# Blocks of 128 rows by seven products in both layers of a routed two-layer network

## The chip, the cores and the metric

The kernel runs on one core of a Trainium2 chip. The metric is the device time of one execution in microseconds; the kernel before takes 626.38 us, the median of 3 runs (626.19 to 627.47).

## What is computed

An attention with a window of 64 positions feeds a network of eight experts. Each of the 4608 rows (8 sequences of 576) goes through the two matrices of one expert: its own choice, or the expert of the row before where a gate says so. Cut to what matters here:

```python
attn = softmax(q @ k.T / 8, masked to the last 64 positions); x = attn @ v   # x: 8 x 576 rows of 512
logits = x @ w_gate                                     # 8 experts
e = argmax(logits[b, s]) or the row before's e          # by a gate on x @ w_local
h = np.maximum(x[b, s] @ w1[e], 0.0)                    # 512 -> 1024
out[b, s] = p[e] * (h @ w2[e])                          # 1024 -> 512, p = softmax(logits)
```

All of it is in fp32.

## The kernel before

Attention and most of the choice of experts come first; the expert stage writes its first h at 137.9 us of the span and fills the rest. Rows are sorted by expert into blocks that each belong to one expert: blocks of 256 rows, and for what an expert has left over, blocks of 128, 64 and 32 rows. A block's rows are gathered by index (GpSimd issues these transfers), its two weight matrices of 2 MB each come over SyncE's queue into a ring of four tiles, and its results are scattered by index to the output.

In method `run` a fixed list gives the order of blocks. With the number of rows in brackets, after three blocks of 256 it is: 256, 256, [128], 256, [32], 256, [128], 256, 256, [128], 256, [32], 256, [128], 256, 256, [64], 256, 256, 256, [64]. So four blocks of 128 rows are computed, each with a block of 256 before it and one behind it. A 32-row block is not computed on its own: its products are put between those of the 256-row block ahead of it.

A block of 256 rows does each layer by seven products of half-size matrices instead of eight (the Winograd form of Strassen's scheme). In each layer the stationary and the moving operand are cut into quarters; VectorE makes four sums of quarters on either side, TensorE does seven products, and ScalarE and VectorE put the products together:

- `prepare` makes four sums of x (`xs`, by `right`) and four of W1 (`ws`, by `left`), the last two of W1 later (`rest`, `more`);
- `big_hidden` starts with `prepare2`, four sums of W2 (again named `ws`, L1326), then does the products L1363. ScalarE saves three interim results (`keep`, L1370); VectorE's adds (L1375) and ScalarE's relu (L1376) make h. The fifth and the seventh product accumulate into the same PSUM tile `px`, which the second VectorE add reads in between. At the end `halves` makes four sums of h (`hs`, L1312);
- `big_result` does the products L1414, ScalarE scales interim results (`kept`, L1420), VectorE finishes the output (L1425).

`hooks` are pieces of other work that `big_result` calls between its products: the rest of the next block's sums, or the products of a 32-row block and the turning of the rows of the block behind that. Turning is VectorE's transpose, L1283.

A block of 128 rows does its layers directly: in `hidden` 32 matmuls of 128 columns (L1514) and two relus (L1525 on VectorE, L1527 on ScalarE), in `result` 8 matmuls of 512 columns (L1566). Blocks of 64 rows use the same methods with 64-wide column halves of the array, two matmuls side by side (L1514 at 64x64, L1544).

In this stage the order on each engine is the order of the code: a manual schedule covers TensorE, VectorE, ScalarE, GpSimd and SyncE, so an engine that waits holds everything behind it. `pace` ties a gather or a scatter to the end of a product; `late` keeps a block's last scatter back into the next block.

## Time and profile before

| | |
|---|---|
| median of 3 runs | 626.38 us (626.19 to 627.47) |
| the profiled execution: its time, its span | 627.78 us, 626.0 us |
| granted TensorE clock, mean | 0.999 |
| PE busy | 600.5 us (96%) |
| VectorE (DVE) busy | 403.2 us (64%) |
| ScalarE (ACT) busy | 200.5 us (32%) |
| GpSimd (POOL) busy | 271.4 us (43%) |
| HBM traffic | 264 GB/s over the span |

The span runs from the first to the last instruction of one profiled execution. In a row of the timeline stand the start in us, the length, the engine, the line, the operation, what it writes and reads, the shape, the number of records, and in brackets the idle time ahead of it and what ended it. An fp32 matmul leaves two records, so the 32 matmuls of L1514 in one block are x64. Matmuls are pipelined: the time that a group takes from the array is read from its start to the next group's start, not from its length. Lengths on VectorE and ScalarE overlap by some 0.1 us when the next instruction needn't wait for the one before.

### The profile page before, as it was taken

How to read it: one execution, taken by the hardware profiler on the slowest of the kernel's cores; microseconds unless marked ns; L12 is line 12 of the kernel's file. 1: busy time of each engine (PE TensorE's matmuls, PEld its weight loads, DVE VectorE, ACT ScalarE, POOL GpSimd, SP SyncE). 2: the span in 40 equal slices, each digit the busy share in tenths (PEclk: the TensorE clock that was granted, in tenths of full speed). 3: DMA queues.
4: the chain of work that ended last, by engine and by line, in shares of the span. 5: the costliest groups of instructions: out<-in, count | busy, mean ns of one | idle time of the engine just before them, and what ended most of it. 6: DMA issues, size and time to landing. Idle time of an engine off the chain costs nothing. (4 is left out here: it accounts for less than half of the span.)

```text
span 626.0 us, 15072 instructions
## 1 busy us (share of the span) xinstructions
PE 600.5 (96%) x6253; PEld 528.9 (84%) x6253; DVE 403.2 (64%) x757; ACT 200.5 (32%) x368; POOL 271.4 (43%) x261
## 2 busy tenths in 40 slices
PE   7888988999999999999999999999999999999995
PEld 6677766788889999979899799978997998999994
DVE  6567579888996767347381885183926763886730
ACT  3766755722382232203130123112221322123120
POOL 4432111622102567437146775175275866452001
PEclk9999999999999999999999999999999999999999
DMA  8999998787945557476967866687768656955601
GB/s 328 401 415 407 365 378 284 273 304 250 385 153 186 190 210 281 170 272 246 394 245 259 321 198 217 230 314 300 299 239 316 256 189 223 403 193 208 233 18 40
DMA packets 31880, 165.80 MB, mean 265 GB/s; under 512 B 10531, under 2 KB 12217, under 8 KB 22586
## 3 DMA queue, kind: packets, MB, share of 16 engines
q1 hardware_dynamic: 20394, 135.54, 58.6%
q0 software_dynamic: 11408, 29.20, 13.0%
q8 instruction: 51, 0.84, 0.5%
q14 instruction: 27, 0.22, 0.1%
HBM read 145.52 MB, written 19.59 MB: 264 GB/s over the span
## 5 line engine op out<-in xcount | busy, mean ns | idle before, releaser
L1184 POOL DMA_INDIRECT xg<-xs,g x118 | 134.2, 1138 | 46.0 <-issue 25.3
L1494 POOL DMA_INDIRECT out_dram<-y,idx x36 | 41.1, 1142 | 161.3 <-DVE y L1425 68.5
L1414 PE MATMUL hp<-ws,hs 128*128 128x256 f32 x384 | 88.9, 380 | 0.0
L1414 PEld LDWEIGHTS hp<-ws,hs 128*128 128x128 f32 x384 | 72.5, 190 | 10.9 <-issue 1.2
L1363 PE MATMUL hp<-xs,ws 128*128 128x128 f32 x672 | 79.7, 275 | 0.0
L1363 PEld LDWEIGHTS hp<-xs,ws 128*128 128x128 f32 x672 | 77.3, 192 | 0.1
L1425 DVE SCALAR_TENSOR_TENSOR y<-hp,pws,kept 128x256 f32<-128x256 f32 x48 | 23.2, 482 | 68.2 <-issue 41.2
L1514 PE MATMUL hp<-xt,w 128*64 128x64 f32 (+2 forms) x640 | 66.2, 276 | 0.0
L1514 PEld LDWEIGHTS hp<-xt,w 128*128 128x128 f32 (+1 forms) x640 | 60.8, 170 | 4.1 <-issue 0.7
L1414 PE MATMUL hp<-w,h 128*128 128x256 f32 x256 | 60.5, 379 | 0.0
L1375 DVE TENSOR_TENSOR h<-hp,keep 128x512 f32<-128x512 f32 x42 | 28.6, 689 | 43.9 <-PE hp L1363 43.1
L1363 PEld LDWEIGHTS hp<-xt,w 128*128 128x128 f32 x448 | 53.2, 192 | 2.7 <-issue 2.3
L1363 PE MATMUL hp<-xt,w 128*128 128x128 f32 x448 | 54.7, 275 | 0.0
L394 PEld LDWEIGHTS sp<-w 64*64 64x64 f32 x1296 | 39.1, 135 | 16.2 <-issue 11.2
L1414 PEld LDWEIGHTS hp<-w,h 128*128 128x128 f32 x256 | 47.3, 190 | 5.7
L425 ACT ACTIVATE p<-sp 128x512 f32<-128x512 f32 x72 | 39.1, 596 | 37.1 <-PE sp L394 34.8
L440 PE MATMUL xo<-vb,p 128*64 128x74 f32 (+1 forms) x576 | 44.0, 228 | 6.9 <-DVE x L450 3.0
L394 PE MATMUL sp<-w 64*64 64x128 f32 (+1 forms) x1296 | 45.1, 267 | 5.7 <-issue 4.5
L430 DVE TENSOR_TENSOR p<-p,mask 128x1024 f32<-128x1024 f32 x29 | 35.8, 1235 | 22.4 <-ACT p L425 22.3
L1184 POOL DMA_INDIRECT pws<-xw,gx x40 | 44.3, 1107 | 13.2 <-issue 8.5
L440 PEld LDWEIGHTS xo<-vb,p 128*64 128x64 f32 x576 | 38.3, 136 | 12.6 <-issue 5.2
L1376 ACT ACTIVATE h<-h 128x512 f32<-128x512 f32 x42 | 26.3, 630 | 60.1 <-DVE h L1375 60.1
(287 smaller groups left out, 977.5 us busy)
## 6 DMA issues: line engine op xcount, KB each, us to landing
w<-in_w_dram SPq DMA_DIRECT2D x22, 2048.0 KB, 9.4
w<-in_w1t_dram SPq DMA_DIRECT2D x20, 2048.0 KB, 8.7
w<-in_kq_dram SPq DMA_DIRECT2D x17, 1024.0 KB, 11.2
w<-in_w_dram SPq DMA_DIRECT2D x24, 512.0 KB, 8.5
xs<-x POOLq DMA_DIRECT2D x9, 1024.0 KB, 5.9
va<-in_v_dram SPq DMA_DIRECT2D x5, 1184.0 KB, 7.5
vtt<-in_vt_dram SPq DMA_DIRECT2D x5, 1024.0 KB, 6.2
va<-in_v_dram SPq DMA_DIRECT2D x3, 1040.0 KB, 15.5
```

The source lines that it names most:

```text
L394: nc.tensor.matmul(sp[j][c * WIN:(c + 1) * WIN, a:b], lhsT=kt[h, hp, block * WIN:(block + 1) * WIN], rhs=qt[h, hp, a:b], start=not biased, ...
L425: nc.scalar.activation(p[:, j], sp[j], Act.Exp, scale=DH ** -0.5)
L430: masked.append(nc.vector.tensor_tensor(p, p, m.to_broadcast([P, 2, SC]), op=Alu.mult))
L440: nc.tensor.matmul(xo[par * WIN:(par + 1) * WIN, j, s * VW:s * VW + n], lhsT=p[:, j, b * WIN:(b + 1) * WIN], rhs=w[:, s, 2 * hp + j, :n], ...
L1184: return self.nc.gpsimd.indirect_dma_start(out=out, out_offset=None, in_=table[:rows, :], in_offset=bass.IndirectOffsetOnAxis(ap=idx, axis=0))
L1363: mm = nc.tensor.matmul(out[:, m, :], lhsT=a[:, kk, m * P:(m + 1) * P], rhs=b[:, kk, :], start=start and m + kk == 0, stop=stop and (m, kk ...
L1375: nc.vector.tensor_tensor(o, x, y, op=add)
L1376: nc.scalar.activation(o, x if y is None else o, Act.Relu)
L1414: mm = nc.tensor.matmul(out, lhsT=a[:, m, :], rhs=b[:, m, :], start=start and m == 0, stop=stop and m == FK // 2 - 1, skip_group_check=True)
L1425: nc.vector.scalar_tensor_tensor(o, x, pw[i], y2, Alu.mult, Alu.add)
L1494: return self.nc.gpsimd.indirect_dma_start(out=self.out[:, :], out_offset=bass.IndirectOffsetOnAxis(ap=st["idx"][:, s:s + 1], axis=0), in_ ...
L1514: mm = nc.tensor.matmul(hp[a, i, :], lhsT=st["w1"][:, kk, m * P:(m + 1) * P][:, a], rhs=st["xt"][:, kk, :n], start=(kk == 0), stop=(kk == ...
```

## The change

Blocks of 128 rows (`n < KINDS[1]`) now have `fast1` and `fast2` set too, so both their layers go by seven products. Where rows and hidden columns are halved, a block of 128 rows leaves 64 on the stationary or the moving side, so the products run on 64-wide column halves of the array (`c` in `big_hidden`). The second layer has a method of its own, `small_result`: in its first three passes (`r1` to `r3`) the two halves of the array do two different products at once, in the fourth (`r4`) they share the seventh. Results in the upper partitions are moved by ScalarE copies, eight small VectorE adds put the output together, and ScalarE scales it by the gate's weight at the end (`store`). The hooks of `small_result` turn and prepare the block behind.

The second part concerns a 256-row block that stands behind a 32-row block (`after`): W2's fourth sum is left out of `prepare2` and made behind h's four sums.

```diff
-        st.update(..., fast1=len(slots) == 2 and n not in PLAIN1,
-                  fast2=len(slots) == 2 and n not in PLAIN2)
+        st.update(..., fast1=n < KINDS[1] and n not in PLAIN1,
+                  fast2=n < KINDS[1] and n not in PLAIN2)
+        st["wide"] = P if st["big"] else HF
...
     def right(self, name, b, marks=(), rest=False):
...
+            if o is t4 and rest:
+                continue
...
     def prepare2(self, st, marks=()):
-        st["w2t"] = self.right("ws2", w2, marks)
+        st["w2t"] = self.right("ws2", w2, marks, "after" in st)
...
     def big_hidden(self, st, step):
...
             for m in range(n):
                 for kk in range(DK // 2):
-                    mm = nc.tensor.matmul(out[:, m, :], lhsT=a[:, kk, m * P:(m + 1) * P], rhs=b[:, kk, :], ...)
+                    for f in range(0, P, c):
+                        mm = nc.tensor.matmul(out[f:f + c, m, :], lhsT=a[:, kk, m * P + f:m * P + f + c],
+                                              rhs=b[:, kk, :], ...)
...
-        self.halves(st)
+        if st["fast2"]:
+            self.halves(st)
+        if "after" in st:
+            t, b = st["w2t"], st["w2q"]
+            nc.vector.tensor_tensor(t[3], b[1][0], t[1], op=Alu.subtract)
...
+    def small_result(self, st, hooks):
...
+        def both(out, *pairs):
+            for m in range(FK // 2):
+                for part, (x, z) in zip((lo, hi), pairs):
+                    mm = nc.tensor.matmul(out[part], lhsT=x[:, m, :], rhs=z[:, m, :], ...)
+            self.pace(mm)
...
+        both(r1, (a[0][0], b[0][0]), (a[0][1], b[1][0]))
+        nc.scalar.copy(g[lo], r1[hi])
+        nc.scalar.copy(u[lo], r1[lo])
+        plus(y[lo, :w], u[lo], g[lo])
+        hook()
+        both(r2, (s[1], t[1]), (s[2], t[2]))
+        plus(v[lo], r2[lo], u[lo])
+        nc.scalar.copy(y[hi, w:], r2[hi])
+        nc.scalar.copy(g[hi], v[lo])
+        hook()
+        both(r3, (s[3], b[1][1]), (s[0], t[0]))
+        nc.scalar.copy(g[lo], r3[hi])
+        plus(v[hi], y[hi, w:], g[hi])
+        plus(y[hi, w:], r3[hi], v[hi])
+        plus(v[lo], v[lo], g[lo])
+        plus(y[lo, w:], r3[lo], v[lo])
+        hook()
+        both(r4, (a[1][1], t[3][:, :, w // 2:]), (a[1][1], t[3][:, :, :w // 2]))
+        nc.scalar.copy(u[hi, :w // 2], r4[lo])
+        plus(y[hi, :w // 2], r4[hi], v[hi, :w // 2])
+        plus(y[hi, w // 2:w], u[hi, :w // 2], v[hi, w // 2:])
+        for _ in range(3):
+            hook()
+
+        def store():
+            nc.scalar.activation(y, y, Act.Copy, scale=st["pw"][0])
+            return self.scatter(st, 0, y)
...
+            if jobs[i]["fast2"] and not jobs[i]["big"]:
+                after, left = jobs[i + 1], []
+                self.result(jobs[i], step, ((lambda: self.turn(after, False, True)),
+                                            (lambda: left.append(self.prepare(after, True))),
+                                            (lambda: None), (lambda: left.pop()())))
+                continue
...
                 after = jobs[i + 2]
+                after["after"] = True
```

In `small_result`, `a` and `s` are h's quarters and sums, `b` and `t` W2's. `a[0][1]` is the quarter of h that the hidden layer's seventh product gives.

The order on TensorE at the first block of 128 rows. Before (rows here count matmuls):

```order
L1414 MATMUL hp<-ws_3408,h 128x256 x4
L1514 MATMUL hp<-xt,w 128x128 x32
L1566 MATMUL yp<-w,h 128x512 x8
L1363 MATMUL hp<-xt,w 128x128 x8
```

With the change:

```order
L1425 MATMUL hp<-ws_3408,h 128x256 x4
L1370 MATMUL hp<-xt,w 64x64 x16
L1370 MATMUL hp<-xs,ws_3507 64x64 x32
L1370 MATMUL hp<-xt,w 64x64 x16
L1370 MATMUL hp<-xs,ws_3507 64x64 x16
L1370 MATMUL hp<-xt,ws_3507 64x64 x16
L1370 MATMUL hp<-xs,w 64x64 x16
L1482 MATMUL hp<-w,h 64x256 x8
L1482 MATMUL hp<-ws_3570,hs 64x256 x8
...
L1482 MATMUL yp<-ws_3570,h 64x128 x8
```

Forty matmuls have become 144 smaller ones: seven hidden products of 16 each, then r1 to r4 of 8 each (r3 stands in eight rows, of which none is shown). The line numbers of the products move from L1363 and L1414 to L1370 and L1425.

The order on VectorE behind that block, where the next block of 256 rows is turned and prepared. Before:

```order
L1525 TENSOR_SCALAR h<-hp 128x4x128
L1283 STREAM_TRANSPOSE xt<-xg 128x4x4x32 x2
L1326 TENSOR_TENSOR xs<-xt 128x256
...
L1312 TENSOR_TENSOR ws_3611<-w,ws_3611 128x1024
L1326 TENSOR_TENSOR ws_3640<-w 128x1024
...
L1326 TENSOR_TENSOR ws_3640<-w,ws_3640 128x1024
L1375 TENSOR_TENSOR h<-hp,keep_3658 128x4x128
L1375 TENSOR_TENSOR h<-hp,keep_3671 128x4x128
```

With the change:

```order
L1487 TENSOR_TENSOR y<-kept_3723,kept_3725 64x256
L1284 STREAM_TRANSPOSE xt<-xg 128x4x4x32 x2
L1487 TENSOR_TENSOR kept_3724<-hp,kept_3723 64x256
L1330 TENSOR_TENSOR xs<-xt 128x256
...
L1314 TENSOR_TENSOR ws_3758<-ws_3758,w 128x1024
L1487 TENSOR_TENSOR kept_3724<-y,kept_3725 64x256
...
L1487 TENSOR_TENSOR y<-kept_3723,kept_3724 64x128
L1314 TENSOR_TENSOR ws_3758<-w 128x1024
...
L1330 TENSOR_TENSOR ws_3798<-w,ws_3798 128x1024
L1382 TENSOR_TENSOR h<-hp,keep_3816 128x4x128
L1382 TENSOR_TENSOR h<-hp,keep_3830 128x4x128
```

The eight small adds (L1487) stand among the transposes and sums of the next block, the first one ahead of the transposes, six between the second and the third sum of W1; the last two rows are the first two adds of the next block's hidden layer, which follow all of it.

The order on VectorE in the first block behind a 32-row block, with the change:

```order
L1330 TENSOR_TENSOR ws_4040<-w 128x1024
L1382 TENSOR_TENSOR h<-hp,keep_4057 128x4x128
...
L1314 TENSOR_TENSOR hs<-h,hs 128x512
L1407 TENSOR_TENSOR ws_4040<-w,ws_4040 128x1024
```

Before, the row of L1407 stood ahead of the add that is now the second row here (as L1326).

More of the change, by code (lines that the diff above doesn't have):

```diff
@@ L1214, in rows @@
                 slots = range(HF0 + n - KINDS[2], HF0 + n - KINDS[2] + 1)
[L1215 to L1216 removed]
+        st.update(x=[], slots=slots, idx=idx, rows=P, big=len(slots) == 2, fast1=n < KINDS[1] and n not in PLAIN1,
+                  fast2=n < KINDS[1] and n not in PLAIN2)
+        st["wide"] = P if st["big"] else HF
         if n >= KINDS[2]:
@@ L1329, in sums @@
     def sums(self, name, a):
-        t = self.one.tile([P, 4, a[0][0].shape[1], a[0][0].shape[2]], F32, name=name)
-        return [t[:, i] for i in range(4)]
+        n, c = a[0][0].shape[1:]
+        t = self.one.tile([P, 4, n, max(c, P)], F32, name=name)
+        return [t[:, i, :, :c] for i in range(4)]
     def prepare2(self, st, marks=()):
         st["w2q"] = w2 = quarters(st["w2"], FK, D)
-        st["w2t"] = self.right("ws2", w2, marks)
+        st["w2t"] = self.right("ws2", w2, marks, "after" in st)
     def halves(self, st):
@@ L1352, in big_hidden @@
         a, s, b, t = st["wq"], st["ws"], st["xq"], st["xt"]
-        self.prepare2(st)
+        if st["fast2"]:
+            self.prepare2(st)
+        n, c = FK // 2, st["wide"]
         st["h"] = h = self.wk.tile([P, FK, BIG], F32, name="h", bufs=1)
-        st["hq"] = hq = quarters(h, FK, BIG)
-        n = FK // 2
-        pz, py, px = (self.ps_h.tile([P, n, P], F32, name="hp") for _ in range(3))
+        st["hq"] = hq = quarters(h[:, :, :2 * c], FK, 2 * c)
+        pz, py, px = (self.ps_h.tile([P, n, P], F32, name="hp")[:, :, :c] for _ in range(3))
         def product(out, a, b, start=True, stop=True):
@@ L1362, in product @@
                 for kk in range(DK // 2):
-                    mm = nc.tensor.matmul(out[:, m, :], lhsT=a[:, kk, m * P:(m + 1) * P], rhs=b[:, kk, :],
-                                     start=start and m + kk == 0,
-                                     stop=stop and (m, kk) == (n - 1, DK // 2 - 1), skip_group_check=True)
+                    for f in range(0, P, c):
+                        mm = nc.tensor.matmul(out[f:f + c, m, :], lhsT=a[:, kk, m * P + f:m * P + f + c],
+                                              rhs=b[:, kk, :], start=start and m + kk == 0,
+                                              stop=stop and (m, kk) == (n - 1, DK // 2 - 1), skip_group_check=True)
             self.pace(mm)
         def keep(i, x):
-            o = self.one.tile([P, n, P], F32, name=f"keep{i}")
+            o = self.one.tile([P, n, P], F32, name=f"keep{i}")[:, :, :c]
             nc.scalar.copy(o, x)
@@ L1451, in big_result, with hook, plus @@
             self.scatter(st, 1, y[1])
+    def small_result(self, st, hooks):
+        nc, add = self.nc, Alu.add
+        hooks = iter(hooks)
+        def hook():
+            next(hooks, lambda: None)()
+        a, s, b, t = st["ha"], st["hs"], st["w2q"], st["w2t"]
+        w, lo, hi = D // 2, slice(HF), slice(HF, P)
+        r3, r2, r1 = (self.ps_h.tile([P, D], F32, name="hp")[:, :w] for _ in range(3))
+        r4 = self.ps_y.tile([P, D], F32, name="yp")[:, :w // 2]
+        y = self.wk.tile([P, D], F32, name="y")
+        u, v, g = (self.one.tile([P, w], F32, name=f"kept{i}") for i in range(3))
+        def both(out, *pairs):
+            for m in range(FK // 2):
+                for part, (x, z) in zip((lo, hi), pairs):
+                    mm = nc.tensor.matmul(out[part], lhsT=x[:, m, :], rhs=z[:, m, :], start=m == 0,
+                                          stop=m == FK // 2 - 1, skip_group_check=True)
+            self.pace(mm)
+        def plus(o, x, z):
+            nc.vector.tensor_tensor(o, x, z, op=add)
+        both(r1, (a[0][0], b[0][0]), (a[0][1], b[1][0]))
[24 more added lines that the diff above has]
+            return self.scatter(st, 0, y)
+        if st.pop("later", None):
+            self.late = store
+        else:
+            store()
     def quarter(self, st):
```

9 lines of the change are left out of this document (5 added, 4 removed).

## The prediction

> **What bounds the kernel now.** I read the page's busy shares and slices first, then TensorE's timeline around one 128-row block, then the busy time of each engine in that block and in the block behind it.
>
> ```profile
> PE 600.5 (96%) x6253; PEld 528.9 (84%) x6253; DVE 403.2 (64%) x757; ACT 200.5 (32%) x368; POOL 271.4 (43%) x261
> PEclk9999999999999999999999999999999999999999
> ```
>
> TensorE is busy 96% of the span at full granted clock. Its timeline (start, length, group) shows the second of the four 128-row blocks, L1514 and L1566, between two 256-row blocks:
>
> ```profile
> 334.31 1.89 PE L1414 MATMUL hp<-ws,h 128*128 128x256 f32 x8
> 336.03 7.31 PE L1514 MATMUL hp<-xt,w 128*128 128x128 f32 x64
> 343.18 7.03 PE L1566 MATMUL yp<-w,h 128*128 128x512 f32 x16
> 350.05 1.95 PE L1363 MATMUL hp<-xt,w 128*128 128x128 f32 x16
> 351.83 3.74 PE L1363 MATMUL hp<-xs,ws 128*128 128x128 f32 x32
> ...
> 360.76 1.95 PE L1363 MATMUL hp<-xs,w 128*128 128x128 f32 x16
> 362.55 1.89 PE L1414 MATMUL hp<-w,h 128*128 128x256 f32 x8
> ```
>
> No row carries an idle note: each group starts where the one before has issued its last matmul. So TensorE's own work sets the pace, and less of it is worth its full time, as long as nobody makes TensorE wait. The engine that could is VectorE. The table by stage (length; then busy time of PE, PEld, DVE, ACT, POOL) for this block and the 256-row block behind it:
>
> ```profile
> 336.03:350.05 14.02, 14.02 (x82) 10.19 (x81) 6.57 (x10) 1.07 (x2) 9.29 (x9) 1.00 0.85 315
> 350.05:374.64 24.59, 24.59 (x170) 23.14 (x168) 19.43 (x26) 6.35 (x11) 18.81 (x17) 1.00 0.69 240
> ```
>
> VectorE works 6.57 of 14.02 us in the 128-row block and 19.43 of 24.59 in the other: 26.0 of 38.6 together. The 12.6 us left over are what the change can use.
>
> **The change part by part.** *TensorE, both layers.* The nearest rows are those of a 64-row block, which already runs 64-wide column halves of the array:
>
> ```profile
> 528.77 1.89 PE L1414 MATMUL hp<-ws,h 128*128 128x256 f32 x8
> 530.59 3.95 PE L1514 MATMUL hp<-xt,w 128*64 128x64 f32 x128
> 534.37 3.63 PE L1544 MATMUL yp<-w,h 128*64 128x256 f32 x32
> 537.93 2.05 PE L1363 MATMUL hp<-xt,w 128*128 128x128 f32 x16
> 539.82 3.74 PE L1363 MATMUL hp<-xs,ws 128*128 128x128 f32 x32
> ```
>
> From 530.59 to 534.37 are 128 records (two per matmul): 29.5 ns each. A new hidden product has 16 matmuls, 32 records, 0.945 us; seven are 6.62 us, where L1514 took 343.18 − 336.03 = 7.15. From 534.37 to 537.93 are 32 records of 256 columns and one change of width: 0.108 us each, so r1, r2 and r3 (16 records each) take 1.735 us, and r4 with half the columns about 0.94 (16 records, bounded by 0.87 and 1.0). That is 6.15 us for L1566's 6.87. A change of width costs 0.09: L1414 begins at 528.77, its eight records take 1.73 (334.31 to 336.03 has the same eight in 1.72), and L1514 begins at 530.59, not 530.50. The same shows from 537.93 to 539.82, 1.89 for what takes 1.78 at 350.05. Each block now has two changes. In the Trainium skill, TensorEngine Tiling, Key Properties says that a change of tiling mode drains TensorE, which speaks against this change; it gives no price, the trace's 0.09 stands for the drain, and by it the sum is the same. By TensorE alone a block would take 6.62 + 6.15 + 0.18 = 12.95 us for 14.02.
>
> *A wait inside the block.* r1's second half multiplies h's quarter that the hidden layer's seventh product makes, right before it. TensorE must wait for ScalarE's relu of that quarter.
>
> ```profile
> 352.03 0.59 ACT L1370 COPY keep<-hp 128x512 f32<-128x512 f32 x1 [1.09 <-PE hp L1363]
> L1466 ACT ACTIVATE qh<-yp 128x256 f32<-128x256 f32 x2 | 0.8, 383 | 2.8 <-PE yp L1462 2.8
> L354 ACT COPY vb<-r 64x288 f32<-64x288 f32 x5 | 2.0, 406 | 0.0
> L356 ACT COPY va<-r 128x288 f32<-128x288 f32 x5 | 2.1, 418 | 0.1
> ```
>
> ScalarE starts 0.20 us after TensorE's next product could (352.03 against 351.83). A relu of 128x256 out of PSUM takes 0.38. With 0.04 back to TensorE (below) this is 0.62, of which r1's first matmul hides 0.22: a hole of 0.40 us. If ScalarE is held by the relus ahead of it, it is up to 0.4 more. 64 partitions cost as much as 128 (406 and 418 ns at 288 columns).
>
> *VectorE.* Its rows behind the same block in the kernel before, and the small forms:
>
> ```profile
> 343.98 1.29 DVE L1283 STREAM_TRANSPOSE xt<-xg 128x512 f32<-128x512 f32 x2
> 345.31 0.42 DVE L1326 TENSOR_TENSOR xs<-xt 128x256 f32<-128x256 f32 x1
> ...
> 346.78 1.22 DVE L1312 TENSOR_TENSOR ws<-w 128x1024 f32<-128x1024 f32 x1
> ...
> 349.18 1.22 DVE L1312 TENSOR_TENSOR ws<-w 128x1024 f32<-128x1024 f32 x1
> ...
> 351.45 1.22 DVE L1326 TENSOR_TENSOR ws<-w 128x1024 f32<-128x1024 f32 x1
> ...
> 354.98 1.22 DVE L1326 TENSOR_TENSOR ws<-w,ws 128x1024 f32<-128x1024 f32 x1
> ...
> 374.84 1.23 DVE L1326 TENSOR_TENSOR ws<-w 128x1024 f32<-128x1024 f32 x1 [0.25 <-PE hp L1414]
> ```
>
> ```profile
> L1326 DVE TENSOR_TENSOR xs<-xt 128x256 f32<-128x256 f32 x28 | 11.8, 420 | 0.7
> L1525 DVE TENSOR_SCALAR h<-hp 128x256 f32<-128x256 f32 x4 | 1.7, 425 | 9.3 <-PE hp L1514 9.3
> ```
>
> From start to start: two transposes 1.2 (1.33 when the next needs them), four xs sums 1.47 (345.31 to 346.78), the first two sums of W1 2.40, the last two 2.27, four sums of W2 4.67 (351.45 to 354.98, plus 1.14). A 128x256 add is 0.42, 0.34 when the next doesn't need it, and reading PSUM costs nothing more (425 ns). The eight small adds of the new result (64x256, two of them 64x128) stand in no row; below they are bounded by 0.2 us (half, if 64 partitions went at double speed) and 0.55 (if partitions and PSUM added to it), above by nothing in the trace. I take the row of equal length per partition, 0.34 to 0.46, and about 0.2 for the halves. In the Trainium skill, VectorE: DVE Perf Modes, section Side-by-side: where the cycles go, works a time out from the elements that one lane reads plus some 158 cycles, at 0.96 GHz: an estimate of 0.43 us for 256 elements, in which the number of partitions does not appear; by it the sum is the same and the cheap end falls away. No run here shows it for 64 partitions.
>
> Per 128-row block VectorE gains four sums of W1, four of W2, four of x, three adds, four sums of h and the eight adds, and loses one relu. All but W1's and x's sums of the block fall into the two stages of the table: 4.9 + 3 × 0.42 + 4 × 0.42 + about 3 − 0.69 = 10.2 us on top of 26.0, so 36.2 of 37.5. On the average that still just fits. The order does not: VectorE works its list strictly in turn, and I follow it from the block's first possible start on TensorE, T.
>
> - T + 0.2 (374.84 against 374.64): W2's four sums, until 4.87. Then the adds for the hidden layer; the second ends at 5.63, and product 7, which overwrites its input, starts at 0.09 + 6 × 0.945 = 5.76. No wait, 0.13 to spare.
> - TensorE issues r1 at 6.71, has the hole of 0.40, ends r1 at 8.85. ScalarE copies both halves (start 9.05; two of 0.37, the second issued 0.27 behind the first): 9.69.
> - Only then can VectorE go on, at T + 9.73. It now runs without a gap: first add 0.34, two transposes of the next block 1.20, r2's add 0.34, xs 1.47, two W1 sums 2.40, six small adds 2.0, two W1 sums 2.27, W2's four sums 4.67, then the next block's first add 0.60 and second 0.69. That is 15.98 us: T + 25.71.
> - The next block's product 7 must wait for that second add: it starts at T + 25.75. By TensorE's own work it could start at 0.09 + 6.62 + 0.40 + 6.15 + 0.09 + 10.71 (360.76 − 350.05) = 24.06. So TensorE waits about 1.7 us there, in each of the four blocks that follow a 128-row one. Before, the same point lay at 360.76 − 336.03 = 24.73.
>
> So each 128-row block with its successor becomes 25.75 − 24.73 = 1.0 us longer: the 1.1 us won on TensorE and 1.0 more come back as two waits. ScalarE's scaling of the block's output, queued ahead of the next block's second keep, waits for the last small add (T + 17.5) and ends by 18.2; the keep is needed at product 6, after T + 22, so this hides. The third add, relu and sums of h follow by T + 27.7, ahead of the result's second product at 29.3. The scatter that hangs on it blocks GpSimd's list till 18.8; the rows gathered behind it are wanted a block later.
>
> *W2's fourth sum behind a quarter block.* The two blocks behind a quarter block have the same wait today:
>
> ```profile
> 320.72 1.88 DVE L1375 TENSOR_TENSOR h<-hp,keep 128x512 f32<-128x512 f32 x3
> ```
>
> ```profile
> 322.05 2.05 PE L1363 MATMUL hp<-xs,w 128*128 128x128 f32 x16 [0.24 <-DVE h L1375]
> ```
>
> The second add ends at 320.72 + 0.60 + 0.69 = 322.01, and TensorE starts 0.04 later, 0.24 late. One sum of 1.13 us less ahead of it removes this twice: −0.5 us. The sum itself is wanted only by the result's last product, some 10 us on, and hides.
>
> **Sum.** 4 × 1.0 − 0.5 = +3.5 us on the profiled execution's span of 626.0, so 629.5. Its own time is 627.78, the median of the runs 626.38; the span and the median are 0.4 us apart, and I add the difference to the median: 629.9 us.
>
> **The rivals.** *TensorE's saving shows (faster).* If VectorE's run of 16.0 us were 1.7 shorter, the point would fall to 24.06: 4 × 0.67 + 0.5 = 3.2 us won, 623.2 us. The eight adds would have to cost next to nothing; every other term has its row, so this is unlikely. It decides from product 7 of the block behind. *Nothing to see.* The adds at 0.2 us each shorten the run by 0.8: 4 × 0.2 − 0.5, near 626.7. *The adds are dear.* At 0.55 the run is 1.5 longer: 4 × 2.5 − 0.5, 635.9. *The halves do not pair.* L1544 pairs two halves with one stationary operand; r1 to r3 use two different ones. If they ran one after the other, r1 would be 1.74 longer and all behind it: 4 × 2.75 − 0.5, 636.9. L1514's rows, with two stationary operands, pair, which speaks against it. That the change does not reach the chip's program is excluded by the order of instructions.
>
> **How the numbers follow.** Forecast 0.72 (its own range 628.2 to 632.0, from ± 0.05 us on each small add and ± 0.2 on the hole); no difference 0.12; faster 0.06; dear adds 0.06; no pairing 0.04. Within 0.2%, 1.25 us, a measurement here can't tell a change. Slower: 0.72 + 0.10 = 0.82; same 0.12; faster 0.06. The range takes in the near edge of no difference: 627.2 to 632.6.
>
> **What would show it.** In the new profile, product 7 (L1370, xs with w) of the four blocks behind a 128-row one carries a wait of about 1.4 to 2 us for DVE h, and L1482's second matmul one of about 0.4 for ACT h; product 7 behind a quarter block has none; VectorE has no gap between the block's first small add and that product. L1370 at 64x64 takes 0.945 us a product. I am wrong if product 7 doesn't wait, or if the small adds leave 0.3 to 0.46 us.

## The result and the profile after

The kernel with the change takes 643.71 us (641.17 to 647.53), the kernel before beside it 626.29 us: ratio 1.0281, 95% interval 1.0225 to 1.0338. Slower was forecast, but by 3.5 us; it is 17. The profiled execution took 642.56 us, its span is 640.8. In two of the five sets of runs further down the kernel before itself took 638 to 648 us instead of 624 to 632, so a time there is read only as its ratio to that kernel.

From the page: busy times, the granted clock in 40 slices, and the queue of instructions (packets, MB, share):

```profile
PE 606.9 (95%) x7085; PEld 540.4 (84%) x7085; DVE 463.1 (72%) x861; ACT 216.1 (34%) x416; POOL 281.9 (44%) x261
...
PEclk9899999999999999998999899998998999999999
...
q8 instruction: 58, 0.95, 0.6%
```

TensorE is busy 6 us longer and the span 15 us; some slices of the clock have an 8; and there are 58 transfers of instructions, 51 before. The waits of TensorE from 225 us to the end (what waited, for whom; us in total, times, longest), first before, then with the change:

```profile
PE hp L1363 <- DVE h L1375: 0.5, 2, 0.2
```

```profile
PE hp L1370 <- DVE h L1382: 9.0, 4, 2.3
PE hp L1370 <- issue: 3.3, 2, 2.0
```

The two waits before, 0.24 us each, stood behind the quarter blocks (the 32-row blocks). Now product 7, the seventh hidden product, waits four times for VectorE behind the 128-row blocks, and twice TensorE waits for "issue", which is nothing that the profile shows. The six places on TensorE's timeline, in order of time, with product 6 (360.39) ahead of one of them:

```profile
272.81 0.62 PE L1370 MATMUL hp<-xs,w 128*64 128x64 f32 x14 [1.33 <-issue]
...
293.41 3.54 PE L1370 MATMUL hp<-xs,w 128*128 128x128 f32 x16 [2.26 <-DVE h L1382]
...
360.39 1.95 PE L1370 MATMUL hp<-xt,ws 128*128 128x128 f32 x16
364.60 3.60 PE L1370 MATMUL hp<-xs,w 128*128 128x128 f32 x16 [2.26 <-DVE h L1382]
...
431.67 2.52 PE L1370 MATMUL hp<-xs,w 128*128 128x128 f32 x16 [2.26 <-DVE h L1382]
...
483.33 1.04 PE L1370 MATMUL hp<-xt,ws 128*64 128x64 f32 x29 [1.97 <-issue]
...
506.53 2.05 PE L1370 MATMUL hp<-xs,w 128*128 128x128 f32 x16 [2.26 <-DVE h L1382]
```

The waits for VectorE stand where the prediction put them, in the blocks behind the 128-row blocks. But the product behind the wait also takes 3.5 us in two cases and 2.5 in one, where it takes 2 undisturbed (506.53): that is a second loss. The waits for issue, inside the 128-row blocks' products of 64x64, are a third.

The table by stage for the second and the fourth 128-row block and the blocks behind them (length; busy time of PE, PEld, DVE, ACT, POOL; granted clock):

```profile
337.92:351.36 13.44, 13.38 (x290) 11.10 (x289) 10.68 (x20) 4.93 (x13) 10.28 (x9) 1.00 0.86 319
351.36:380.20 28.84, 26.58 (x169) 24.95 (x169) 24.90 (x35) 6.37 (x12) 23.34 (x19) 0.94 0.59 218
...
476.37:493.29 16.92, 14.95 (x290) 13.40 (x289) 10.79 (x20) 4.93 (x13) 11.06 (x10) 0.90 0.76 293
493.29:520.51 27.22, 24.96 (x170) 23.32 (x170) 24.68 (x35) 6.37 (x12) 18.89 (x15) 1.00 0.56 200
```

Undisturbed, the 128-row block takes 13.44 us; before it took 14.01. The block behind takes 27.22 with the wait alone and 28.84 with the wait and half clock; before 24.60. VectorE works 35.6 us in the two, which took 38.6 before.

From each block's first product to the next block's, in us (before: the same in three traces but for the one range given; "again": a second trace of the changed kernel):

| stretch | before | after | again |
|---|---|---|---|
| first 128-row block | 14.01 | 15.12 | 15.53 |
| block behind, with a quarter block | 28.96 | 33.08 | 31.59 |
| block behind the quarter block | 25.05–25.10 | 24.68 | 24.68 |
| second 128-row block | 14.01 | 13.44 | 13.44 |
| block behind | 24.60 | 28.84 | 28.87 |
| third 128-row block | 14.01 | 13.53 | 13.53 |
| block behind, with a quarter block | 28.96 | 33.26 | 31.59 |
| block behind the quarter block | 25.05–25.10 | 24.69 | 24.68 |
| fourth 128-row block | 14.01 | 16.92 | 15.62 |
| block behind | 24.59 | 27.22 | 28.90 |
| first 128-row block to the last product's end | 351.3 | 368.9 | 366.5 |

Ahead of the first 128-row block nothing changed, and the traces of one and the same kernel differ by up to 3 us there; so I compare from that block on. Of the 17.5 us that the profiled execution loses, the wait at product 7 is 4 × 2.63 = 10.5 us (27.22 against 24.59; 0.10 of each is the change from 64-wide to 128-wide products, which falls into this stretch: its first product takes 1.88 us to the next one's start instead of 1.78), the half clock behind it 1.5 + 1.6 + 1.7 = 4.8 (33.08 and 33.26 against 31.59, 28.84 against 27.22), the waits for issue 1.6 + 3.4 = 5.0 (15.12 and 16.92 against 13.5, the second with half clock behind it); the 128-row blocks themselves win 2.1 and the blocks behind the quarter blocks 0.8.

*Why VectorE is later than forecast.* Its timeline behind the second 128-row block, whose first possible start on TensorE is T = 337.83, and ScalarE's two copies of r1 ahead of it:

```profile
347.19 0.37 ACT L1490 COPY kept<-hp 64x256 f32<-64x256 f32 x1 [2.08 <-PE hp L1482]
347.58 0.37 ACT L1491 COPY kept<-hp 64x256 f32<-64x256 f32 x1
```

```profile
347.98 0.42 DVE L1487 TENSOR_TENSOR y<-kept,kept 64x256 f32<-64x256 f32 x1 [1.73 <-ACT kept L1491]
...
351.30 1.22 DVE L1314 TENSOR_TENSOR ws<-w 128x1024 f32<-128x1024 f32 x1
...
353.81 0.42 DVE L1487 TENSOR_TENSOR kept<-y,kept 64x256 f32<-64x256 f32 x1
...
356.20 1.23 DVE L1314 TENSOR_TENSOR ws<-w 128x1024 f32<-128x1024 f32 x1
...
358.47 1.22 DVE L1330 TENSOR_TENSOR ws<-w 128x1024 f32<-128x1024 f32 x1
...
363.25 1.89 DVE L1382 TENSOR_TENSOR h<-hp,keep 128x512 f32<-128x512 f32 x3
```

No idle note from 347.98 on, as forecast. But the run begins at T + 10.15 instead of 9.73, and lasts until 364.56 (product 7's start less the 0.04 us of the forecast), 16.58 us instead of 15.98: the six small adds take 2.39 us (353.81 to 356.20) for 2.0, two sums of W1 2.51 for 2.40, W2's four 4.78 for 4.67.

*The half clock.* The trace's records of half clock in this stage begin at 293.14, 364.82, 433.09 and 484.29 us, each 3.413 us long, and lie 21, 20 and 15 times 3.413 us apart: the granted clock changes on a grid. Two holes of equal length, cut into stretches of 3.4 us along it (the last three figures of a row are clock, DMA share and GB/s):

```profile
361.40:364.80 3.40, 1.14 (x10) 0.95 (x9) 3.37 (x5) 0.82 (x2) 2.79 (x3) 1.00 0.09 25
364.80:368.20 3.40, 3.40 (x17) 3.40 (x17) 2.33 (x4) 1.00 (x2) 2.69 (x3) 0.50 0.27 98
...
504.80:508.20 3.40, 1.67 (x15) 1.67 (x16) 2.67 (x5) 1.82 (x3) 2.79 (x3) 1.00 0.20 61
508.20:511.60 3.40, 3.40 (x19) 3.04 (x18) 3.37 (x6) 1.07 (x2) 2.48 (x4) 1.00 0.67 198
```

The hole ending at 364.60 lies wholly in one stretch, in which TensorE is idle for 2.26 us; the next stretch runs at half clock. The hole ending at 506.53 is cut by the stretch's border, 1.73 us lie behind it, and the clock stays. So the theory that the runs were to test had three parts: VectorE's lateness makes the hole, the place of the hole on this grid decides on half clock, and the waits for issue come from the supply of instructions. The rivals: contention with the loads of weights for the waits for issue, and another cause for half clock.

### The profile page after: what moved, and what is told of

Read it like the earlier page. It is cut to its first block, busy times and chain, and to the rows that moved or that the text cites. A ratio compares the mean times of both kernels' runs of the same rounds, so it can differ in the third digit from the quotient of the medians.

```text
span 640.8 us, 16918 instructions
## 1 busy us (share of the span) xinstructions
PE 606.9 (95%) x7085; PEld 540.4 (84%) x7085; DVE 463.1 (72%) x861; ACT 216.1 (34%) x416; POOL 281.9 (44%) x261
## 5 line engine op out<-in xcount | busy, mean ns | idle before, releaser
L1184 POOL DMA_INDIRECT xg<-xs,g x118 | 140.0, 1186 | 43.5 <-issue 26.2
L1370 PE MATMUL hp<-xs,ws 128*128 128x128 f32 (+1 forms) x1056 | 92.3, 256 | 0.0
L1370 PEld LDWEIGHTS hp<-xs,ws 128*128 128x128 f32 (+1 forms) x1056 | 89.2, 172 | 0.1
L1425 PE MATMUL hp<-ws,hs 128*128 128x256 f32 x384 | 88.9, 380 | 0.0
L1425 PEld LDWEIGHTS hp<-ws,hs 128*128 128x128 f32 x384 | 72.6, 190 | 10.9 <-issue 1.2
L1370 PE MATMUL hp<-xt,w 128*128 128x128 f32 (+1 forms) x704 | 64.1, 257 | 0.0
L1370 PEld LDWEIGHTS hp<-xt,w 128*128 128x128 f32 (+1 forms) x704 | 61.0, 172 | 2.8 <-issue 2.4
L1425 PE MATMUL hp<-w,h 128*128 128x256 f32 x256 | 61.9, 385 | 0.0
L1382 DVE TENSOR_TENSOR h<-hp,keep 128x512 f32<-128x512 f32 (+1 forms) x54 | 32.7, 628 | 35.9 <-PE hp L1370 35.8
L1383 ACT ACTIVATE h<-h 128x512 f32<-128x512 f32 (+1 forms) x54 | 30.8, 583 | 77.5 <-DVE h L1382 77.5
L1184 POOL DMA_INDIRECT pws<-xw,gx x40 | 48.2, 1205 | 13.4 <-issue 8.9
L1425 PEld LDWEIGHTS hp<-w,h 128*128 128x128 f32 x256 | 48.5, 195 | 6.0
L1330 DVE TENSOR_TENSOR ws<-w 128x1024 f32<-128x1024 f32 x40 | 49.1, 1229 | 3.6 <-PE hp L1425 2.5
L1330 DVE TENSOR_TENSOR ws<-w,ws 128x1024 f32<-128x1024 f32 x38 | 46.5, 1224 | 0.7
```

Of the source, the lines that this page charges most:

```text
L1184: return self.nc.gpsimd.indirect_dma_start(out=out, out_offset=None, in_=table[:rows, :], in_offset=bass.IndirectOffsetOnAxis(ap=idx, axis=0))
L1330: self.nc.vector.tensor_tensor(o, x, y, op=sub)
L1370: mm = nc.tensor.matmul(out[f:f + c, m, :], lhsT=a[:, kk, m * P + f:m * P + f + c], rhs=b[:, kk, :], start=start and m + kk == 0, stop=sto ...
L1382: nc.vector.tensor_tensor(o, x, y, op=add)
L1383: nc.scalar.activation(o, x if y is None else o, Act.Relu)
L1425: mm = nc.tensor.matmul(out, lhsT=a[:, m, :], rhs=b[:, m, :], start=start and m == 0, stop=stop and m == FK // 2 - 1, skip_group_check=True)
```

## Experiments

**Both kernels again.** No edit.

> The kernel before, unchanged, for a trace of it beside the others of this call: the kernel before took 626 us in its first runs and 638 to 643 us beside the last four experiments. Theory 'TensorE is at times fed slowly with instructions': where it takes over 630 us its trace shows TensorE idle with no releaser for 0.3 to 2 us at a time, 5 to 15 us in all, and no more transfers of instructions than in the first trace (51). Rival 'a lower clock': the mean granted clock is under 0.98 and the idle time as in the first trace.

> The changed kernel, unchanged, beside the kernel before on this chip. Theory 'VectorE is late, half clock in the holes': ratio to the kernel before 1.02 to 1.04 on any chip, with the four waits of 2.3 us for VectorE's h at the seventh product. If the losses of instruction supply grow with the density of instructions, the ratio is above 1.03 where the kernel before is above 635 us. If the moved sums of the runs before gained nothing, this one's ratio is at or under 1.031 (with two sums moved) in the same conditions; if they gained 8 us, it is about 1.043.

The kernel before took 626.18 us, the changed one 645.05, ratio 1.030 (1.027 to 1.033). The second trace is the table's last column: the same four waits of 2.26 us, half clock behind two of them instead of three, and waits for issue of 1.73 and 1.97. In the table by stage, along the grid, one hole with and one without:

```profile
362.20:365.60 3.40, 1.14 (x10) 0.94 (x10) 3.37 (x5) 1.11 (x2) 2.79 (x3) 1.00 0.14 39
365.60:369.00 3.40, 3.40 (x16) 3.31 (x16) 2.03 (x4) 1.23 (x3) 2.49 (x4) 0.50 0.19 66
430.50:433.90 3.40, 1.70 (x15) 1.71 (x16) 2.67 (x5) 1.83 (x3) 2.79 (x3) 1.00 0.26 95
433.90:437.30 3.40, 3.40 (x19) 3.04 (x18) 2.92 (x9) 1.07 (x2) 2.41 (x3) 1.00 0.69 213
```

The kernel before was traced a third time beside later runs:

> The kernel before beside the two. If it takes over 635 us here: its trace shows TensorE's waits without a releaser, 0.3 to 2 us each and 10 to 16 us in all behind the first 240 us, where its first traces show none, with a granted clock of 0.99 and the same 51 transfers of instructions. If it takes 626 us: 351.3 us from the first 128-row block to the end, as in the two traces there are.

It took 627.56 us, and its trace has 351.31 us from the first 128-row block on. What it loses when it takes 640 us is in no trace and stays open.

**The part next to the quarter blocks alone.** The 128-row blocks are left out of both layers' seven products:

```diff
-PLAIN1, PLAIN2 = (-1, -2), ()
+PLAIN1, PLAIN2 = (-1, -2, *tuple(range(KINDS[0], KINDS[1]))), tuple(range(KINDS[0], KINDS[1]))
```

> The kernel before plus one part alone: next to a quarter block W2's fourth sum follows h's four sums; the 128-row blocks stay as in the kernel before in both layers. Theory: the two waits of 0.24 us at the seventh product behind the quarter blocks go, 0.5 us in all: ratio 0.998 to 1.001. Rival 'h's later fourth sum makes the result's seventh product late': ratio above 1.002.

Measured 627.10 us against 627.15, ratio 0.9989 (0.9964 to 1.0014). The two blocks behind the quarter blocks, by stage:

```profile
311.37:335.96 24.59, 24.59 (x169) 23.15 (x168) 16.31 (x21) 6.12 (x11) 13.22 (x12) 1.00 0.69 256
442.13:466.73 24.60, 24.60 (x170) 23.15 (x169) 16.34 (x21) 6.11 (x11) 12.77 (x12) 1.00 0.71 259
```

They take 24.6 us instead of 25.05 to 25.10: the waits printed as 0.24 were worth 0.46 to 0.51 each. So this part wins 0.9 us in the trace; the interval of the runs takes in both that and nothing.

**One layer at a time.** The 128-row blocks by seven products in the first layer alone, with `PLAIN2` as in the edit above and `PLAIN1` as in the changed kernel:

> The changed kernel with the 128-row blocks by seven products in the first layer alone (their second layer as in the kernel before: no small adds, no sums of h and of W2 for them; the next block's turn and sums where the kernel before has them). Theory: VectorE has 13 additions fewer between the 128-row block's products and the next block's seventh product, so that wait is under 0.5 us and no half clock comes from it; what is left is the supply of instructions in the 64x64 products (0 to 3 us a block, more where the kernel before is slow too): ratio 0.995 to 1.015. Rival 'the first layer's sums make VectorE late': the waits of 2 us stay, ratio above 1.02.

Measured 633.67 us, ratio 1.0115 (1.009 to 1.0141). No wait for VectorE is left, and the blocks behind take 28.96 and 24.59 as before. All of the loss is one wait in each of the four 128-row blocks (7.0 us as printed; the trace as a whole loses 5.9 from the first 128-row block on):

```profile
272.42 0.68 PE L1370 MATMUL hp<-xs,w 128*64 128x64 f32 x15 [1.70 <-issue]
...
340.72 0.97 PE L1370 MATMUL hp<-xt,ws 128*64 128x64 f32 x25 [1.97 <-issue]
...
407.24 7.13 PE L1635 MATMUL yp<-w,h 128*128 128x512 f32 x16 [1.58 <-issue]
...
475.16 0.51 PE L1370 MATMUL hp<-xt,ws 128*64 128x64 f32 x10 [1.73 <-issue]
```

In the second layer alone, with `PLAIN1` as in the edit of the part before and `PLAIN2` empty; the plain first layer then has to cut h into quarters at the block's own width:

```diff
-            st["hq"] = quarters(h, FK, BIG)
+            st["hq"] = quarters(h[:, :, :2 * st["wide"]], FK, 2 * st["wide"])
```

> The changed kernel with the 128-row blocks by seven products in the second layer alone (their first layer as in the kernel before: 64 products of 128x128, about 7.1 us instead of 6.6). Theory: VectorE's run behind the first small add has the same work, so the wait of about 2.3 us and the half clock stay in the four blocks; what goes is the wait without a releaser in the 64x64 first-layer products (1.3 us at S19, 2.0 us and a half clock at S22): 643.7 - 5 + 4 x 0.5 = about 640. Rival 'the first layer's added sums are what makes VectorE late': the wait falls under 1 us and the time under 634.

> The 128-row blocks by seven products in the second layer alone, once more, beside a kernel before that may take 626 us. Theory: the second layer brings the whole of the holes (VectorE's sums of h and W2 and the small adds are its) and none of the waits without a releaser; the 128-row blocks last 14.3 us, no less than in the kernel before, the blocks behind them 27.2 (31.6) us or 28.9 (33.1) with half clock: 10.5 us of holes + 1.2 + 2 to 5 of half clock - 0.9 behind the quarter blocks = 638.5 to 642, ratio 1.018 to 1.025. Rival 'the first layer brings a part of VectorE's lateness': holes under 1.5 us, ratio under 1.015.

The first run took 650.94 us against 642.57, ratio 1.0154 (1.0086 to 1.0222), the second 654.11 against 643.89, 1.0149 (1.009 to 1.0208), under the 1.018 expected of it. The stages are clear; from the second run, behind the second and the first 128-row block:

```profile
361.26:388.44 27.18, 25.23 (x170) 23.40 (x170) 24.64 (x34) 6.84 (x13) 17.37 (x15) 1.00 0.61 207
287.76:319.35 31.59, 29.32 (x268) 25.96 (x267) 20.43 (x34) 7.76 (x16) 16.79 (x13) 1.00 0.77 283
```

These are the changed kernel's 27.22 and 31.59 without half clock. So VectorE's lateness comes with the second layer, and the waits at the 64x64 products with the first (the third of them stands right behind these).

**Less in VectorE's run.** W2's third and fourth sums (or the fourth alone) behind h's four in the four blocks behind the 128-row blocks, as the change itself does next to quarter blocks:

```diff
+            if (o is t4 and rest) or (o is t3 and rest > 1):
+                continue
...
+                after["after"] = 2        # the other run: 1
```

> The changed kernel, but in the four blocks behind a 128-row block W2's third and fourth sums follow h's four sums (2.4 us out of VectorE's run that ends ahead of the seventh hidden product). Theory 'VectorE is late' (the seventh product waits for the end of that run, about 2.05 us a block, and TensorE runs at half clock after the hole, another 1.6 in most blocks): the wait of 2.26 us at the seventh product of those blocks is gone or under 0.3, that product takes 1.8 us instead of 3.4, and 8 to 12 of the 17 us go: 630 to 635 us. Rival 'instruction supply' (TensorE's waits without a releaser in the 64x64 products are the main loss): the waits go but the time stays above 637. Rival 'the loss moves': the later sums make h's or the result's fifth product late, the time stays above 637 with new waits at L1425.

> As the run before, but only W2's fourth sum is moved in those four blocks (1.2 us). Theory 'VectorE is late': the wait shrinks to about 1.1 us. If a hole of about 1.2 us is too short to bring the half clock, product seven takes 1.8 us and the time falls by 4 x 1.2 + about 4 = 9 to about 635; if a hole of that size brings it too, it falls by 4.8 only, to about 639. If VectorE's run is not what is waited for, nothing changes: 643.

Beside a kernel before of 642.57 us these took 661.38 (ratio 1.0309, 1.025 to 1.0368) and 662.40 (1.0354, 1.0291 to 1.0416): in the first, the four waits for VectorE's h were gone, but 24 waits for issue of 10.6 us in all had come. Both runs once more, the second of them twice:

> The run with W2's third and fourth sums behind h's four once more, beside a kernel before that may take 626 us this time. Theory 'VectorE is late, half clock in the holes': the blocks behind the 128-row blocks last 24.6 (with a quarter block 29.0) us from their first product to the next block's, as in the kernel before, instead of 27.2 or 28.9 (31.6 or 33.1); that is 10.5 us of holes and 3 to 5 of half clock less: 629 to 631 us, ratio 1.002 to 1.008, the rest being TensorE's waits without a releaser in the 64x64 products (about 2 us each in the first and the fourth 128-row block). Rival 'the first run of this kernel showed its price': ratio about 1.03 again, the 128-row blocks 23 us long.

> W2's fourth sum alone behind h's four in the blocks behind the 128-row blocks, once more. Theory: holes of 1.2 us instead of 2.4, no half clock from them (a stretch of 3.41 us at half clock followed only where TensorE idled at least 1.9 of the 3.41 us ahead of it, 0 of 25 times below 1.8): the blocks behind last 25.9 to 26.1 (30.4 to 31) us; time 632 to 636, ratio 1.008 to 1.015. Rival 'any hole can bring half clock': one or more of these blocks over 27 us.

> W2's fourth sum alone behind h's four in the blocks behind the 128-row blocks, once more and for the same reason. If the kernel before takes 626 us: holes of about 1.2 us and 26.1 us (with a quarter block 30.5) for those blocks, no half clock in them, 633 to 637 us, ratio 1.010 to 1.016. Rival: a block over 27.5 (32) us with half clock.

With the fourth sum alone: 669.44 us beside 643.89 (1.0411, 1.0348 to 1.0474), cut up by waits for issue like the first runs, and then 635.79 us beside 628.09, ratio 1.0143 (1.0103 to 1.0184), as expected; the wait is 1.12 us and no half clock follows it. With both sums: 633.82 us beside 627.22, ratio 1.0101 (1.0068 to 1.0133), 3 us above the expectation. The first row is a stage of the run with one sum moved; the others, two stages and a wait on the timeline, are of the run with both:

```profile
352.26:378.35 26.09, 24.97 (x170) 23.33 (x169) 24.68 (x35) 6.37 (x12) 21.19 (x17) 1.00 0.62 231
```

```profile
353.84:379.14 25.30, 25.21 (x169) 23.24 (x169) 23.95 (x34) 6.40 (x12) 20.43 (x17) 1.00 0.64 239
285.23:315.72 30.49, 29.20 (x268) 25.95 (x268) 20.34 (x34) 7.42 (x15) 12.32 (x11) 1.00 0.76 281
```

```profile
302.81 1.93 PE L1533 MATMUL yp<-w,xt 128*32 128x256 f32 x32 [1.29 <-DVE xt L1284]
```

27.2 (28.8 with half clock) becomes 26.1 and 25.3, so VectorE's run is the cause of the hole. 25.3 is still 0.7 more than 24.6: 0.10 is the change of width, and product 7 and the result's last product each start 0.15 to 0.25 late, with 0.10 more behind each. And 30.49 is not 28.96: the sums that were moved now stand ahead of the turning of the quarter block's rows (L1284), and TensorE waits for that instead. A part of the loss moves.

**Work in the hole.** TensorE multiplies a constant ahead of product 7, with 20 or 7 transposes of 128x128 whose result nobody reads; the wait for VectorE stays:

```diff
+        if "fill" in st:
+            tp = self.ps_t.tile([P, DK, P], F32, name="tp")
+            for _ in range(20):           # the other run: 7
+                nc.tensor.transpose(tp[:, 0, :], self.ident, self.ident)
         product(px, a[1][1], t[3], False)
```

> The changed kernel with 20 transposes of a constant (about 2.2 us of TensorE work whose result nobody reads) ahead of the seventh hidden product in the four blocks behind a 128-row block: the wait for VectorE stays as long, but TensorE is busy in it. Theory 'the idle hole brings the half clock': product seven takes 1.8 us instead of 3.4 in all four, and the time falls by about 4 us, to about 639 to 640. Rival 'the half clock comes from something else (power, the dense 64x64 products)': product seven still takes 3.4 in most blocks and the time is 643 or a little more.

> The run with 20 transposes of a constant ahead of the seventh product once more. Theory 'the idle hole brings the half clock': the blocks behind the 128-row blocks all last 27.2 (31.6) us, none 28.9 (33.1), and no record of half clock stands in them; by that alone the time would be 3 to 5 us under the changed kernel's 644. The 20 transposes also move the places of TensorE's waits without a releaser (they come at every fifth 126 or so products in program order): a wait of about 1.7 us is expected in the third 128-row block too, which had none: 641 to 643 us. Rival 'half clock has another cause': two or three blocks of 28.9 (33.1) us stay.

> The changed kernel with 7 transposes of a constant (0.8 us) ahead of the seventh product behind the 128-row blocks, so that 1.5 to 1.6 us of the hole of 2.4 stay idle. Theory 'a stretch of 3.41 us with over 1.9 us idle is followed by one at half clock': none of these four blocks has half clock, they last 27.2 (31.6) us each, and the time is 638 to 642, as with 20 transposes. Rival 'each hole brings it with some chance': one or two blocks at 28.9 (33.1) us in the trace, time about 643.

> The changed kernel with 7 transposes ahead of the seventh product once more, since the last run of it stood beside a kernel before of 644 us and was cut up by TensorE's waits without a releaser. If the kernel before takes 626 us this time: the four blocks behind the 128-row blocks last 27.2 (31.6) us, none has half clock, 638 to 642 us, ratio 1.018 to 1.024. Rival 'each hole brings half clock with some chance': one or two of them last 28.9 (33.1) us. If the kernel before takes over 635 us again, nothing on this can be read.

The first runs of both stood beside a kernel before of 642.57 and 643.89 us (670.87 us, 1.0482, 1.0408 to 1.0556; 676.33 us, 1.0428, 1.0333 to 1.0524) and are cut up by waits for issue. The second ones took 639.11 us beside 627.22, ratio 1.0198 (1.0164 to 1.0233), and 638.24 us beside 628.09, 1.0169 (1.0133 to 1.0204). With 20 transposes 641 to 643 us had been expected: the third 128-row block has its new wait for issue, but the fourth has lost its own. Neither of these two traces has half clock anywhere in the stages of the table. The stage behind the second 128-row block, with 20 and with 7:

```profile
352.88:380.11 27.23, 27.15 (x190) 25.47 (x190) 24.69 (x35) 6.36 (x12) 22.02 (x18) 1.00 0.59 219
```

```profile
353.36:380.60 27.24, 25.73 (x177) 24.05 (x177) 24.70 (x35) 6.37 (x12) 21.75 (x19) 1.00 0.58 218
```

Both last as long as the stage with the wait alone. So half clock comes from TensorE's idle time, is worth 1.6 us in such a stage, and does not come when 1.50 us of the 2.26 stay idle.

**Other places for the borders of instructions.** 40 transposes of 32x32 at the very start, nothing else:

```diff
     warm(12)
+    r = bank()
+    for _ in range(40):
+        nc.tensor.transpose(r[:QR, :QR], ident[:QR, :QR], ident[:QR, :QR])
```

> The changed kernel with 40 transposes of 32x32 of a constant at the very start, ahead of the first load's arrival, and nothing else. Theory 'blocks of instructions': TensorE's instructions come in pieces of about 126 products, whose borders stand at fixed places of the program; the second border that falls inside a 128-row block's 224 dense 64x64 products costs a wait of 1.3 to 2.0 us there, the first none. 40 products more move all places by 40: the wait in the first such block goes from its product 209 to 169, the second has a new one at 206 and the third at 214, the fourth loses its wait of 1.97 us (at 163). Rival 'contention with the loads of weights at those times': the waits stay in the first and the fourth block, at the same places, and none comes in the second and third.

What this expectation calls products are matmul records of the profile, of which a 128-row block's first layer has 224. In the run with the first layer alone the four waits stand at the records 3778, 4410, 5043 and 5675 of TensorE, five times 126.5 apart; in the changed kernel at 3778 and 5800, sixteen times 126.4. So the borders are 126 records apart, with as many weight loads between them. With 40 records more (lines are 3 higher), 646.02 us, ratio 1.0302 (1.0247 to 1.0357):

```profile
274.16 0.86 PE L1373 MATMUL hp<-xt,ws 128*64 128x64 f32 x22 [2.00 <-issue]
...
346.94 0.74 PE L1373 MATMUL hp<-xs,w 128*64 128x64 f32 x17 [1.71 <-issue]
...
414.45 0.51 PE L1373 MATMUL hp<-xs,w 128*64 128x64 f32 x10 [1.52 <-issue]
```

They stand at records 169, 206 and 214 of the first three blocks, and the fourth has none: four of four as expected. The loads of weights had hardly moved (issued 9.0 and 14.5 us behind the first block's first product, 8.5 to 8.9 and 13.9 to 14.3 in the changed kernel's two traces), so contention with them doesn't choose the places. The traces also show the transfers that bring TensorE's instructions (q8 of the page, 16 KB each). In the nine traces of kernels with 128-row blocks by seven products whose kernel before took 626 to 628 us, each of the 19 waits for issue ends 1.2 to 1.6 us behind the end of such a transfer, whether the wait was 0.8 or 2.5 us long: in the changed kernel's trace one lands at 271.54, and TensorE goes on at 272.81. At the 17 borders that lie 96 to 142 records into such a block and cost nothing, the last transfer had ended 4.2 us or more before.

**A version against both.** Only the second and third 128-row blocks go by seven products, with both sums moved behind them, the part next to the quarter blocks kept, and 100 transposes of 32x32 in place of the 12 at the start. Of the edit, the line that leaves the first and fourth block out:

```diff
-PLAIN1, PLAIN2 = (-1, -2), ()
+PLAIN1, PLAIN2 = (-1, -2, KINDS[0], KINDS[0] + 3), (KINDS[0], KINDS[0] + 3)
```

> A version against both kernels: only the second and third 128-row blocks by seven products (the first and fourth as in the kernel before), W2's third and fourth sums behind h's four in the blocks after them, the move next to the quarter blocks kept, and 100 transposes of 32x32 at the start in place of 12 of 128x128, which puts the borders of the instruction pieces 5 to 15 products ahead of the first dense product. By theory: no wait without a releaser, no hole; 13.5 us instead of 14.0 for two blocks and 0.46 less behind each quarter block: 2.0 us less from the first 128-row block to the end, ratio 0.996 to 0.998 unless the transposes at the start cost more than they replace. Rival: the waits stay or come elsewhere, ratio above 1.000.

Measured 628.13 us, ratio 1.0015 (0.9993 to 1.0036), where 0.996 to 0.998 was expected: not better. The borders did what was asked, and no wait for issue is left. The stages are the second 128-row block, the block behind it, and the block with a quarter block behind the third:

```profile
334.61:348.04 13.43, 13.37 (x289) 11.10 (x288) 10.67 (x20) 4.92 (x13) 8.95 (x8) 1.00 0.89 329
348.04:373.28 25.24, 25.22 (x169) 23.25 (x169) 23.89 (x34) 6.39 (x12) 20.64 (x16) 1.00 0.64 234
411.50:442.02 30.52, 29.39 (x267) 25.96 (x267) 20.56 (x35) 7.41 (x15) 15.83 (x13) 1.00 0.81 303
```

The 0.58 us won in the block are less than the 0.65 and 1.56 lost behind it, of which 0.10 each is the change of width and the rest is waiting for VectorE. In this order of work VectorE has no room for the second layer's sums.

## Why the prediction was right or wrong

Slower came, by the wait that was named. But of the 14 us between the forecast of +3.5 and the trace's +17.5, some 4.2 are that wait, which was mis-sized, 4.8 the half clock behind it and 5.0 the waits for issue; the sum had put the last two at nothing, with no row behind it.

- *What bounds the kernel; TensorE's terms.* Right, but for the fourth pass. Seven hidden products take 6.58 us (337.92 to r1's start at 344.50) for 6.62. The block takes 13.44 and 13.53 where no wait for issue cuts it, and 0.19 more with both changes of width, which fall into its neighbours: 13.63 for 12.95 + 0.40. The term that was too small is r4: from its start to the next product 1.40 us pass, for 0.94.
- *The hole of 0.40 us at r1.* r1's start to r2's is 2.01 us, 1.735 of it work: 0.28. Near enough, though the wait that was to show it on L1482 stands in no row.
- *"VectorE can go on at T + 9.73."* T + 10.15. ScalarE's copies of r1 start 0.31 later than taken (347.19) and 0.39 apart instead of 0.27.
- *"15.98 us without a gap."* Without a gap, but 16.58. The largest part is the six small adds: the four of 64x256 come 0.44 to 0.52 us apart, where 2.0 us for all six leaves 0.40. In two of these distances the next add needs the sum before it; in the other two it doesn't, but works on the other half of the partitions. The last two, where neither holds, do overlap: they are 0.29 us long and come 0.21 apart. Why a change of halves costs as much as a dependence no run here shows.
- *"TensorE waits about 1.7 us, 1.0 us longer with its successor."* This is the step that was mis-sized. VectorE is done at T + 26.73 instead of T + 25.71, and product 7 starts at 364.60 where TensorE's own work allows 362.17 (360.39 + 1.78): 2.4 us. The pair is 13.44 + 27.22 − 38.61 = 2.05 us longer. A margin that is the difference of two sums of 25 us doubled with an error of 1.0 in one of them; over four blocks that is 4.2 us of the miss.
- *Half clock.* Missing. The hole was priced at its length; behind it TensorE loses another 1.5 to 1.7 us in three cases of four (two of four in the second trace). Work put in the hole removed it.
- *Supply of instructions.* Missing. The 29.5 ns a record came from a stretch of 128 records in the 64-row block, too short for a border far into it; the 224 of the new stretch hold one in some blocks, and 1.3 to 2.0 us of waiting with it. Shifting the borders moved the waits.
- *"−0.5 for the two blocks behind quarter blocks."* Right in kind, 0.9 in size. The idle time printed in a row is less than its price: behind 0.24 product 7 starts 0.40 late (322.05 against 319.86 + 1.79 in the first trace of the kernel before), behind 2.26 it starts 2.43 late, and in both cases the product after it starts another 0.10 later.
- *What would show it.* Product 7 waits (2.26, above the 1.4 to 2 given) and doesn't wait behind quarter blocks, VectorE's run has no gap, 64x64 products take 0.94: all seen. The wait on L1482 was not. The range of 627.2 to 632.6 was made from unknown durations alone, so both missing mechanisms lay outside it.
- *The rivals.* TensorE's saving is there in undisturbed 128-row blocks, but only 0.3 to 0.4 us a block with the changes of width. Dear adds came nearest in mechanism: the adds cost 0.4 us a block more than forecast, not 1.5. The halves pair: r2, r3 and r4 start 2.01, 1.73 and 1.72 us after the pass before.

## What to carry to other kernels

Where the forecast is a small difference of two long runs, a wait at the end of one is best given with the whole error of both, and its price is more than its length. TensorE's idle time had a second price here that depended on where the hole fell on a grid of 3.4 us; a few matmuls of a constant in the hole removed it. The price of many small matmuls in a row is not only their time one by one: count the instructions, and look for borders of instruction blocks inside the dense stretch.

## What the chip showed that was not expected

*Half clock after less than 3.4 us of idle time.* The granted clock changes on a grid of 3.413 us. From the rows behind 225 us of the same nine traces I added up TensorE's idle time in each stretch of this grid: all eight with 1.92 to 2.27 us were followed by a stretch at half clock, none of 37 with 0.7 to 1.79, and of two in between the one with 1.89 was and the one with 1.90 was not. So in these traces a little over half of a stretch idle was enough. In the Trainium skill, TensorE: Matmul & The Clock Gate, Part 1: The HAM clock gate, the clock falls to half after at least one idle window, the window being 3413 ns and free-running, and the section HAM oscillation — how this bites in real kernels gives as the rule "no PE-idle gaps >~3.4µs". The traces agree with the window, but holes of 2.4 us bring half clock here.

*Waits at borders of instructions.* In the same traces, a border at record 96 to 142 of a 128-row block's dense stretch cost nothing (17 cases, nor did any at record 0 to 87), one at 163 to 225 cost 0.8 to 2.5 us (19). The records come 29.5 ns apart there, so 126 pass in 3.7 us. So where the stretch was dense for 160 records or more ahead of a border, the next instructions came too late. In the Trainium skill, Runtime: NRT & Kernel Launch, section Instruction fetch mechanics, instructions come in blocks of 256 and the crossing is "mostly hidden"; the distance of the borders agrees, the cost does not for such dense products. A transfer itself takes about 1 us (271.54 − 270.60 = 0.94 for the one above). Why it starts no earlier, and what fills the 1.2 to 1.6 us from its end to the next product, stays open.

*Waits for issue in many pieces.* In most traces taken beside a kernel before of 638 to 648 us (there is none of that kernel itself) TensorE waits for issue in places every four to ten records, mostly 0.3 to 0.5 us each time, above all inside the 128-row blocks. The run with 20 transposes was 1.0482 of the kernel before there, 1.0198 otherwise. The cause is open.
